# Loading x straight into the first transform's operand, at 128 elements a position instead of 130

## The chip, the cores and the metric

The kernel runs on one core of a Trainium2 chip. The metric is the device time of one execution in microseconds (us). The core has a matrix engine (TensorE, PE in the profile; its weight loads are PEld), VectorE (DVE), ScalarE (ACT), GpSimd (POOL) and SyncE (SP). In this kernel GpSimd and SyncE mostly issue DMA transfers.

## The reference

Two layers in a row, for x of 8 batches, 5696 positions and 128 channels. The first is a long convolution along the positions, the second a spectral mix of the first 64 modes, with a residual and a ReLU.

```python
L = 2 * S                                   # S = 5696
y = np.fft.irfft(np.fft.rfft(x, n=L, axis=1) * np.fft.rfft(h, n=L, axis=0)[None], n=L, axis=1)[:, :S]
X = np.fft.rfft(y, axis=1)                  # second layer, on y
Y[:, :64] = (Xr @ w_r - Xi @ w_i) + 1j * (Xr @ w_i + Xi @ w_r)    # for each mode
u = y + np.fft.irfft(Y, n=S, axis=1)
out = u + np.maximum(u @ w_ch, 0)
```

Inputs and output are float32; the kernel works in 16-bit floats (fp16) in its on-chip memory.

## The kernel before, in words

A sequence of 5696 positions is seen as 89 rows (`NQ`) of 64 positions (`J`). One row lies on one partition of the on-chip memory, so that partition q holds positions 64 q to 64 q + 63, with 128 channels each. The Fourier transform is split into a first transform over the 89 rows, done for each of the 64 places in a row, and a second one over the 64 places, done for each of 90 frequencies (`NK`). The batches are worked off in four pairs (`NP`).

The tile `Xin` (`x_sb`, L221) is the first transform's operand. It has 2 x 64 positions on each partition, and a position takes `XS = D + 2 = 130` elements: 128 channels and 2 unused ones.

The first transform of a pair is 32 calls of `a_tile` (L444). Each has four matmuls, and each matmul loads one channel of all 128 positions (two batches of 64) from Xin as its weights: 128 columns that lie `XS` elements apart. It then runs the 180 columns of the table `F1` through them. The results are evacuated into `As`, in turn by ScalarE and VectorE.

The second part of a pair is a loop of 26 ticks (`tick`, L619). Up to tick 22, each tick transforms four frequencies from As (`second`), multiplies them by the filter's spectrum on VectorE (`products`, tiles `U`), runs the inverse over the 64 places (weights `Wc`), evacuates to `Zs` or `Zt`, and stores to a scratch in device memory (`zscr`); the modes for the second layer are summed on the way (weights from Zs and Zt, table `G`). As becomes free from the front: after tick t, the part for that tick's frequencies is not read any more.

The next pair's x is loaded during the same loop. It comes in eight pieces (two batches, four pieces of 16 places, `XC = 4`), each as two DMA transfers from GpSimd's queue (9 rows and 80 rows; `x_load`, L353), which turn float32 into fp16. Piece i is issued in tick 2 (i + 1) (L638), after that tick's products and after the reads of As so far. It lands in a room `Xt` (`x_st`, L241), which lies over the part of As that has become free. Later, in the ticks that the table `XPLACE` gives (L611), VectorE copies each room into Xin (`x_place`, L360): 16 runs of 128 elements on 89 partitions, each run at a step of 130. The next pair's first transform begins in ticks 22 to 25 (six calls of `a_tile`, the table `border`, L528) and is finished after the loop (26 calls, L699).

The first pair's x lands in other rooms (`Xr`, L240) and is copied to Xin by the same `x_place` (L438) while the filter h is transformed. Its first transform is interleaved with the first matmuls of the filter's second transform (L680). The rows of Xin from partition 64 on are set to zero once at the start (L344).

Nobody writes waits by hand: every operation names what it reads and writes, and a recorder (L21) works out which operations on other queues it must wait for. A token such as `("xin", i)` stands for piece i of Xin. An engine works its own instructions off in the order in which they are recorded.

Of the kernel before, what the change touches and what calls it, by code (L numbers as in the profile page):

```python
# [4 lines left out]
P = 128  # L5
F16 = mybir.dt.float16
# [117 lines left out]
def bass_long_conv_fft__then__afno_spectral_mix_kernel(nc, x, h, moe_w_r, moe_w_i, moe_w_ch, out):  # L124
    B, S, D = x.shape
    M = moe_w_r.shape[0]
    assert D == P and M == 64 and B == 8
    J = 64
    NQ = S // J
# [3 lines left out]
    NP = B // 2  # L133
# [72 lines left out]
    def at(name, cols, dt, off):  # L206
        return nc.alloc_sbuf_tensor_at(name, [P, cols], dt, offset=off)

    def take(nbytes):
        off = (cur[0] + 31) // 32 * 32  # L210
        cur[0] = off + nbytes
        assert cur[0] <= end, (cur[0], end)
        return off

    AW, HW, GW = NK * 2 * D, NK * D, (NK // 2 + 1) * P
    a_as = take(AW * 2)
    a_sb = at("As", AW, F16, a_as)
    XS = D + 2
    XW = 2 * J * XS
    a_x = take(XW * 2)  # L220
    x_sb = at("Xin", XW, F16, a_x)  # L221
    a_m = take(MW * 2)
    m_sb = at("M", MW, F16, a_m)
# [5 lines left out]
    NU, NXS, NZ, NZX = 3, 2, 6, 10  # L229
# [7 lines left out]
    XC = 4  # L237
    XN = J // XC
    XB = XN * D
    x_all = at("Xr", 2 * XC * XB, F16, a_h)  # L240
    x_st = [at(f"Xt{i}", XB, F16, a_as + i * XB * 2) for i in range(2 * XC)]  # L241
    u_s = [at(f"U{i}", 2048, F16, a_st + i * 4096) for i in range(NU)]
    x_s = [at(f"Xs{i}", 1024, F16, a_st + NU * 4096 + i * 2048) for i in range(NXS)]
    z_s = [at(f"Zs{i}", 1024, F16, a_st + NU * 4096 + (NXS + i) * 2048) for i in range(NZ)] + \
# [1 line left out]
    f1_sb = at("F1", 2 * NK, F16, take(2 * NK * 2))  # L246
# [3 lines left out]
    xt = at("XT", B * XTW, F16, a_g + GW * 2 + 2048 * (NZX - NZ))  # L250
# [31 lines left out]
    def ap(t, row, p0, n, off, dims):  # L282
        return bass.AP(t, p0 * row + off, [[row, n]] + [list(d) for d in dims])
# [8 lines left out]
    R = Recorder(nc)  # L292
# [23 lines left out]
    def dma(eng, dst, src, ring, reads=(), writes=(), after=()):  # L316
        R.add(eng, lambda h_: h_.dma_start(dst, src), reads, writes, ring=ring, after=after)  # L317
# [32 lines left out]
        dma("gpsimd", bass.AP(h_in, o_, dims), bass.AP(h.tensor, h.offset + o_, dims), "x", (), [("hin", i)])  # L350
    HT = [("hin", i) for i in range(len(h_parts))] + [("hz",)]

    def x_load(g_, i, dst, toks, after=()):  # L353
        b, c_ = divmod(i, XC)
        for p_, (q0, n) in enumerate(((QA, NQ - QA), (0, QA))):
            dma("gpsimd", bass.AP(dst, q0 * XB, [[XB, n], [1, XB]]),
                bass.AP(x.tensor, x.offset + (2 * g_ + b) * S * D + q0 * J * D + c_ * XB, [[J * D, n], [1, XB]]),
                "x", (), [toks[p_]], after=after)

    def x_place(i, src, toks):  # L360
        R.add("vector", lambda e: e.tensor_copy(bass.AP(x_sb, i * XN * XS, [[XW, NQ], [XS, XN], [1, D]]),  # L361
                                                src),
              list(toks) + XZ, [("xin", i)])

    def w_pieces():
        out_ = []
# [10 lines left out]
    RA = 2 * XC * XB  # L377
# [8 lines left out]
            dma("gpsimd", bass.AP(x_all, (b_ * XC + c_) * XB, [[RA, QA], [1, XB]]),  # L386
                bass.AP(x.tensor, x.offset + b_ * S * D + c_ * XB, [[ROW, QA], [1, XB]]), "x", (), [("xr", b_ * XC + c_, 1)])
    XZ = [("xz",)]
    XIN = [("xin", i) for i in range(2 * XC)]
    XR = [[("xr", i, p_) for p_ in range(2)] + [("xl", 0), ("xl", 1)] for i in range(2 * XC)]  # L390
    MP = 6
    GP = 2 * KT
# [30 lines left out]
    for j in range(16):  # L423
        t = turns("h", [0, 2, 4])
        for i in range(4):
            d = 4 * j + i
            mm(pv(t + i // 2, (i % 2) * 2 * NK, [[1, 2 * NK]]),
               ap(hp_sb, 2 * J * HS, 0, P, d, [[HS, 2 * J]]), f1_sb[:, :], True, True,
               [("hz",), ("hp", d // DC), ("f1",)], [bank(t + i // 2)])
        for i in range(4 if j < 15 else 26):  # L430
            mm(pv(6 + i % 2, 0, [[1, 2 * NK]]), f1_sb[:, 0:P], f1_sb[:, :], True, True, [("f1",)], [bank(6 + i % 2)])
        evac(bass.AP(ah_sb, 4 * j, [[HW, P], [DH, 2 * NK], [2, 2], [1, 2]]),
             pv(t, 0, [[1, 2 * NK], [512, 2], [2 * NK, 2]]),
             [bank(t), bank(t + 1)], [("ah", j)], 1.0 / 64,
             eng="vector" if j in (3, 7) else "scalar")
        if j % 2:
            i = j // 2 % 2 * XC + j // 4
            x_place(i, bass.AP(x_all, i * XB, [[RA, NQ], [D, XN], [1, D]]), XR[i])  # L438

    HP = [("hz",), ("hp", 0), ("hp", 1)]  # L440
    AHT = [("ah", j) for j in range(16)]
    AST = [("as", j) for j in range(33)]

    def a_tile(j, slots, eng=None):  # L444
        t = turns("s", slots) if len(slots) > 1 else slots[0]
        for i in range(4):
            d = 4 * j + i
            mm(pv(t + i // 2, (i % 2) * 2 * NK, [[1, 2 * NK]]),
               ap(x_sb, XW, 0, P, d, [[XS, 2 * J]]), f1_sb[:, :], True, True,
               XIN + XZ + [("f1",)], [bank(t + i // 2)])  # L450
        if eng == "both":
            for i, e in enumerate(("vector", "scalar")):
                evac(bass.AP(a_sb, 4 * j + 2 * i, [[AW, P], [D, 2 * NK], [1, 2]]), pv(t + i, 0, [[1, 2 * NK], [2 * NK, 2]]),
                     [bank(t + i)], [("as", j + i)], 1.0 / 64, eng=e, after=once(("hp", j), HP))
            return
        evac(bass.AP(a_sb, 4 * j, [[AW, P], [D, 2 * NK], [2, 2], [1, 2]]),
             pv(t, 0, [[1, 2 * NK], [512, 2], [2 * NK, 2]]),
             [bank(t), bank(t + 1)], [("as", j)], 1.0 / 64, eng=eng, after=once(("hp", j), HP))
# [149 lines left out]
              bk + [("h", t, 0), ("h", t, 1, 0), ("h", t, 1, J)], [("u", i)])  # L608

    Z_OLD = [("ag", k) for k in range(NS, NS + 8 * (NZX - NZ))]  # L610
    XPLACE = [9, 10, 12, 15, 16, 18, 20, 22], [9, 10, 13, 14, 17, 18, 20, 22]  # L611

    def zroom(g_, s_):
        return (s_ - 2 * NZ) % NZX if g_ == 0 and s_ >= 2 * NZ else s_ % NZS[g_]

    def xtok(n):
        return [("xt", n, p_) for p_ in range(2)]

    def tick(g_, t):  # L619
        if g_ + 1 < NP:  # L620
            for i in range(2 * XC):
                if t == XPLACE[g_ > 0][i]:
                    x_place(i, bass.AP(x_st[i], 0, [[XB, NQ], [D, XN], [1, D]]), xtok(i))
        with_h = with_h_at(g_, t)
        if t < NT:
            of_two = t > 0 and twin(g_, t - 1)
            if not of_two:
                second(g_, t)
            products(g_, t, slot_of(g_, t))
            if twin(g_, t):  # L630
                second(g_, t + 1)
                if straight(g_, t):
                    copied(g_, t + 1, slot_of(g_, t + 1))
        drain = list(border[t]) if t in border and g_ + 1 < NP else []
        if drain and t >= NT:
            j, sl, e = drain.pop(0)
            a_tile(j, [sl], e)
        if g_ + 1 < NP and t % 2 == 0 and 0 < t <= 4 * XC:  # L638
            i = t // 2 - 1
            x_load(g_ + 1, i, x_st[i], xtok(i), [("u", t % NU)] + AST)  # L640
        if LC <= t < NT + LC:
            s_ = t - LC
            n = len(ticks[s_])
            i, zi = s_ % NU, zroom(g_, s_)
            zb = [turns("z", ZBANK) for b in range(2)]
            for b in range(2):
                for r in range(2):
                    mm(pv(zb[b], 0, [[1, n * D]]), (W1, W2)[r], u_s[i][:, r * 1024 + b * 512:r * 1024 + b * 512 + n * D],
                       r == 0, r == 1, [("u", i), ("wc",)], [bank(zb[b])])
                evac(bass.AP(z_s[zi], b * D, [[1024, P], [2 * D, n], [1, D]]),  # L650
                     pv(zb[b], 0, [[D, n], [1, D]]), [bank(zb[b])], [("zs", zi, b)], eng="scalar",
                     after=once(("zx", zi, b), Z_OLD) if zi >= NZ else ())
            zo = (g_ * NK + KT * s_) * P * 256
            dma("sync", bass.AP(zs, zo, [[256, P], [P * 256, n], [1, 256]]),
                bass.AP(z_s[zi], 0, [[1024, P], [256, n], [1, 256]]), "z",
                [("zs", zi, 0), ("zs", zi, 1)], [("zd", g_, s_)])
            if drain and t >= NT:
                j, sl, e = drain.pop(0)
                a_tile(j, [sl], e)
        if LM <= t < NT + LM:  # L660
            s_ = t - LM
            zi = zroom(g_, s_)
            for i, k in sorted(enumerate(ticks[s_]), key=lambda q: (s_ > 0 or q[1] != 1, q)):
                for b in range(2):
                    if k % 2:
                        o, off, n, sl = pv(MB, b * P, [[1, P]]), (k + 1) // 2 * P, P, (k + 1) // 2
                    else:
                        ms, off = even[k]
                        n, sl = 2 * len(ms), 0
                        dims = [[M, 2]] if len(ms) == 1 else [[ms[1] - ms[0], 2], [M, 2]]  # L670
                        o = pv(MB, b * P + ms[0], dims)
                    mm(o, z_s[zi][:, i * 256 + b * P:i * 256 + b * P + P], g_sb[:, off:off + n],
                       k == 1 and b == 0, k == NK - 1 and b == 1, [("g", sl // GP), ("zs", zi, b)], [bank(MB)])
        if drain and t < NT + LM - 1:
            j, sl, e = drain.pop(0)
            a_tile(j, [sl], e)
        if with_h:
            filter_tick(t + LH, [2, 3])
# [216 lines left out]
```

## Time and profile before

| what | value |
|---|---|
| three timed runs | 391.25, 392.1 and 393.78 us; median 392.1 us |
| span of the profiled execution, first to last instruction | 390.0 us |
| its own time beyond the span | not listed; the runs' median is 2.1 us above the span |
| mean granted TensorE clock | 0.981 of full speed |
| HBM read, written | 70.61 MB, 51.12 MB |

The span has these stages: loading and transforming h, and the first pair's first transform (to about 46 us); the first pair's ticks (to about 100 us); the second and the third pair (to about 156 and 212 us); the last pair's ticks (to about 263 us); and then the inverse transform with the second layer and the output.

In the views, a group of instructions is given as line, engine, operation, `out<-in` by the program's tile names, and the shape. The number after x counts them. In a timeline, the first number is the start in us and the second the duration in us of the instructions merged into the line; brackets give how long the engine was idle before, and what ended that.

### The profile page before, as it was taken

To read this page: it belongs to the slowest core of one execution; us is meant where nothing else is said; L and a number is where in the kernel's file an instruction comes from. 1 tells how busy PE (TensorE), PEld (TensorE's weight loads), DVE (VectorE), ACT (ScalarE), POOL (GpSimd) and SP (SyncE) were. 2 spreads that over 40 slices of the span, in tenths; PEclk is the share of its full clock that TensorE was granted. 3 is DMA by queue.
4 is the path that set the end of the run, shared out by engine and by line. 5 is a ranking of instruction groups with operands and counts; after the bars stand their busy time and mean duration, and the time that the engine had idled before them with its cause. 6 is when DMAs were issued, how large, how long until landed. Compare 5 with 4: busy or idle time off the path is not lost.

```text
span 390.0 us, 12484 instructions
## 1 busy us (share of the span) xinstructions
PE 363.7 (93%) x5346; PEld 280.4 (72%) x5346; DVE 304.9 (78%) x346; ACT 311.0 (80%) x489; POOL 84.3 (22%) x134
## 2 busy tenths in 40 slices
PE   7699999998989999989998989999999999999992
PEld 7597766654866666866666856668898988988871
DVE  3358789988998999998998997875437767777784
ACT  8278689888889998989996999995457676777783
POOL 8500013220453320643210411319300000000000
PEclk9899999999999999999999999998899999999997
DMA  7998559999598998999996849999999999999967
GB/s 146 184 284 327 143 98 257 272 253 281 93 138 188 225 254 235 98 129 198 226 260 193 86 134 383 301 337 394 405 400 394 418 405 409 405 406 379 360 276 287
DMA packets 87089, 103.94 MB, mean 267 GB/s; under 512 B 22823, under 2 KB 72615, under 8 KB 83563
## 3 DMA queue, kind: packets, MB, share of 16 engines
q1 hardware_dynamic: 62523, 67.73, 49.7%
q0 software_dynamic: 24512, 35.43, 43.5%
q8 instruction: 42, 0.69, 0.7%
q14 instruction: 12, 0.10, 0.1%
HBM read 70.61 MB, written 51.12 MB: 312 GB/s over the span
## 4 chain that ended last, share of the span: by engine, by line
PE 68%; DMA 9%; DVE 8%; ACT 8%; issue 3%; POOL 1%; SPq 0%; DVEq 0%; ACTq 0%; POOLq 0%
PE ps L320 68%; DMA Hin<-in_h_dram 3%; DVE As L314 2%; DMA Hs<-Hs 2%; DMA zscr<-Zs 2%; DMA Xt<-in_x_dram 2%; ACT As L310 2%; DVE U L599 2%; ACT Zs L308 1%; DVE U L607 1%; ACT Xs L308 1%; ACT R L829 1%; ACT Zt L308 1%; ACT UT L308 1%; DVE Hs L312 1%
## 5 line engine op out<-in xcount | busy, mean ns | idle before, releaser
L607 DVE TENSOR_TENSOR U<-Xs,Hs 128x2048 f16<-128x2048 f16 (+1 forms) x73 | 86.9, 1193 | 16.0 <-ACT Xs L308 11.3
L320 PE MATMUL ps<-U,Wc 128*128 128x512 f16 (+1 forms) x368 | 94.3, 376 | 1.2 <-DVE U L607 0.6
L308 ACT CAST Xs<-ps 128x1024 f16<-128x1024 f32 (+1 forms) x77 | 74.9, 977 | 12.3 <-PE ps L320 7.4
L308 ACT CAST Zs<-ps 128x512 f16<-128x512 f32 (+1 forms) x134 | 70.7, 597 | 4.1 <-PE ps L320 2.5
L830 DVE TENSOR_TENSOR O<-ps,R 128x512 f32<-128x512 f32 x81 | 52.5, 684 | 19.9 <-ACT R L829 12.5
L314 DVE TENSOR_SCALAR As<-ps 128x720 f16<-128x720 f32 x70 | 58.1, 884 | 6.7 <-PE ps L320 5.9
L829 ACT ACTIVATE R<-ps 128x512 f32<-128x512 f32 x96 | 50.9, 573 | 14.1 <-PE ps L320 13.7
L320 PE MATMUL ps<-F,Xin 128*128 128x180 f16 x512 | 53.8, 249 | 4.1 <-DVE Xin L361 1.9
L320 PE MATMUL ps<-As,M 64*128 64x128 f16 x1440 | 50.3, 217 | 4.5 <-DVE U L599 2.9
L320 PEld LDWEIGHTS ps<-F,Xin 128*128 128x128 f16 x512 | 44.5, 155 | 12.8 <-DVE As L314 3.6
L320 PE MATMUL ps<-WI,UT 128*128 128x256 f16 x360 | 51.8, 279 | 0.5 <-DVE O L830 0.4
L310 ACT ACTIVATE As<-ps 128x720 f16<-128x720 f32 (+1 forms) x61 | 45.8, 770 | 7.0 <-PE ps L320 5.7
L320 PEld LDWEIGHTS ps<-U,Wc 128*128 128x128 f16 x368 | 28.4, 97 | 30.7 <-ACT Zs L308 5.3
L317 POOL DMA_DIRECT2D Xt<-in_x_dram x48 | 25.9, 544 | 105.2 <-PE ps L320 100.3
L320 PEld LDWEIGHTS ps<-As,M 64*128 64x128 f16 x1440 | 40.6, 94 | 10.7 <-DVE U L599 3.6
L308 ACT CAST UT<-ps 128x712 f16<-128x712 f32 x40 | 30.0, 752 | 19.0 <-PE ps L320 18.1
L320 PEld LDWEIGHTS ps<-WI,UT 128*128 128x128 f16 x360 | 39.3, 152 | 4.2 <-issue 1.7
L320 PE MATMUL ps<-IBs,C 128*128 128x356 f16 x128 | 40.5, 326 | 0.6
L320 PEld LDWEIGHTS ps<-G,Zs 128*128 128x128 f16 x524 | 26.6, 96 | 15.0 <-ACT Zs L308 2.5
L607 DVE TENSOR_TENSOR U<-ps,Hs 128x2048 f16<-128x2048 f32 x15 | 34.2, 2283 | 0.0
L320 PE MATMUL ps<-G,Zs 128*128 128x128 f16 (+2 forms) x524 | 33.0, 192 | 0.1
L312 DVE CAST UT<-ps 128x712 f16<-128x712 f32 x24 | 21.4, 890 | 9.8 <-PE ps L320 9.8
(87 smaller groups left out, 510.4 us busy)
## 6 DMA issues: line engine op xcount, KB each, us to landing
out_dram<-O SPq DMA_DIRECT2D x39, 512.0 KB, 10.2
zscr<-Zs SPq DMA_DIRECT2D x64, 256.0 KB, 7.4
Xt<-in_x_dram POOLq DMA_DIRECT2D x24, 320.0 KB, 7.0
zscr<-Zt SPq DMA_DIRECT2D x24, 256.0 KB, 6.9
W<-wscr POOLq DMA_DIRECT2D x4, 1024.0 KB, 8.0
M<-cM POOLq DMA_DIRECT2D x5, 720.0 KB, 20.5
ZT0a<-zscr SPq DMA_DIRECT2D x3, 1024.0 KB, 13.1
Hs<-Hs SPq DMA_DIRECT2D x44, 64.0 KB, 5.9
```

The lines of the kernel that those rows point to most:

```text
L308: R.add(e, lambda h_: h_.copy(dst, src), reads, writes, after=after)
L310: R.add(e, lambda h_: h_.activation(dst, src, COPY, scale=scale), reads, writes, after=after)
L312: R.add(e, lambda h_: h_.tensor_copy(dst, src), reads, writes, after=after)
L314: R.add(e, lambda h_: h_.tensor_scalar_mul(dst, src, scale), reads, writes, after=after)
L317: R.add(eng, lambda h_: h_.dma_start(dst, src), reads, writes, ring=ring, after=after)
L320: R.add("tensor", lambda h_: h_.matmul(o, l, r, start=st, stop=sp), reads, writes)
L599: R.add("vector", lambda e, b=b, s_=s_: e.tensor_tensor(bass.AP(u_s[i], b * 512, [[2048, P], [1024, 2], [1, n * D]]), s_, hv, MULT), [tok, ...
L607: R.add("vector", lambda e: e.tensor_tensor(uv, src, hv, MULT), bk + [("h", t, 0), ("h", t, 1, 0), ("h", t, 1, J)], [("u", i)])
L829: R.add("scalar", lambda e: e.activation(rv, src_r, RELU), bk, [("r", i % NR)], after=once(("r", i % NR), G_ALL + XTT + [("y", 0), ("y", 1 ...
L830: R.add("vector", lambda e: e.tensor_tensor(ov, src_u, rv, ADD), bk + [("r", i % NR)], [key + (h_,)], after=once(key, old))
```

## The change

The rooms Xt, their tokens and the table XPLACE go. `x_load` writes the two transfers of a piece directly into Xin, whose positions are now 128 elements apart, so that the 16 positions of a piece are one run of 2048 elements on each partition. A load is issued in the same tick as before, after that tick's products; it no longer waits for the reads of As. It has to wait for the matmuls that read the old x, as the recorder finds. Each piece has two tokens in place of one, for its two transfers, so the first transform of the second to fourth pair waits for 16 transfers where it waited for VectorE's copies. The first pair's copies stay, with contiguous destinations. The memory that Xin takes, and the place of everything behind it, stays the same (512 bytes are left free).

```diff
-    XS = D + 2
-    XW = 2 * J * XS
-    a_x = take(XW * 2)
+    XW = 2 * J * D
+    a_x = take(XW * 2 + 512)
...
-    x_st = [at(f"Xt{i}", XB, F16, a_as + i * XB * 2) for i in range(2 * XC)]
...
-    def x_load(g_, i, dst, toks, after=()):
+    def x_load(g_, i, after=()):
         b, c_ = divmod(i, XC)
         for p_, (q0, n) in enumerate(((QA, NQ - QA), (0, QA))):
-            dma("gpsimd", bass.AP(dst, q0 * XB, [[XB, n], [1, XB]]),
+            dma("gpsimd", bass.AP(x_sb, q0 * XW + i * XB, [[XW, n], [1, XB]]),
                 bass.AP(x.tensor, x.offset + (2 * g_ + b) * S * D + q0 * J * D + c_ * XB, [[J * D, n], [1, XB]]),
-                "x", (), [toks[p_]], after=after)
+                "x", (), [("xin", i, p_)], after=after)
 
     def x_place(i, src, toks):
-        R.add("vector", lambda e: e.tensor_copy(bass.AP(x_sb, i * XN * XS, [[XW, NQ], [XS, XN], [1, D]]),
-                                                src),
-              list(toks) + XZ, [("xin", i)])
+        R.add("vector", lambda e: e.tensor_copy(bass.AP(x_sb, i * XB, [[XW, NQ], [1, XB]]), src),
+              list(toks) + XZ, [("xin", i, 0), ("xin", i, 1)])
...
-    XIN = [("xin", i) for i in range(2 * XC)]
+    XIN = [("xin", i, p_) for i in range(2 * XC) for p_ in range(2)]
...
-               ap(x_sb, XW, 0, P, d, [[XS, 2 * J]]), f1_sb[:, :], True, True,
+               ap(x_sb, XW, 0, P, d, [[D, 2 * J]]), f1_sb[:, :], True, True,
...
-    XPLACE = [9, 10, 12, 15, 16, 18, 20, 22], [9, 10, 13, 14, 17, 18, 20, 22]
...
-        if g_ + 1 < NP:
-            for i in range(2 * XC):
-                if t == XPLACE[g_ > 0][i]:
-                    x_place(i, bass.AP(x_st[i], 0, [[XB, NQ], [D, XN], [1, D]]), xtok(i))
...
-            x_load(g_ + 1, i, x_st[i], xtok(i), [("u", t % NU)] + AST)
+            x_load(g_ + 1, i, [("u", t % NU)])
```

## The prediction

> **What bounds the kernel now.** I read the profile in this order: the busy shares of the page, the groups of instructions kept apart by shape, the view of tile Xin, narrow stretches of the timeline, and a table by stage.
>
> ```profile
> PE 363.7 (93%) x5346; PEld 280.4 (72%) x5346; DVE 304.9 (78%) x346; ACT 311.0 (80%) x489; POOL 84.3 (22%) x134
> ```
> TensorE is busy for 93% of the span and VectorE for 78%. TensorE is the bound on average; VectorE matters only where TensorE waits for it.
>
> ```profile
> L320 PEld LDWEIGHTS ps<-F,Xin x512: 145/152/188, 28.7 to 222.6; 128*128 128x128 f16 x171
> L361 DVE COPY Xin<-Xt x24: 677/682/690, 66.5 to 206.6; 89x2048 f16<-89x2048 f16 x24
>   PE ps L320: 1.9, 3
> ```
> From the view of tile Xin (ns min/median/max; the last line, under "who waited for it", is us, times): the 24 copies that go are 24 x 0.682 = 16.4 us of VectorE, but TensorE waited for one only 3 times, 1.9 us in all. The change also touches 512 weight loads that read Xin.
>
> ```profile
> 126.41 1.21 DVE L607 TENSOR_TENSOR U<-Xs,Hs 128x2048 f16<-128x2048 f16 x1
> 127.54 0.68 DVE L361 COPY Xin<-Xt 89x2048 f16<-89x2048 f16 x1
> 128.15 1.22 DVE L607 TENSOR_TENSOR U<-Xs,Hs 128x2048 f16<-128x2048 f16 x1
> ...
> 131.25 2.28 DVE L607 TENSOR_TENSOR U<-ps,Hs 128x2048 f16<-128x2048 f32 x1
> ...
> 138.29 2.28 DVE L607 TENSOR_TENSOR U<-ps,Hs 128x2048 f16<-128x2048 f32 x1
> ```
> ```profile
> 228.64 2.28 DVE L607 TENSOR_TENSOR U<-ps,Hs 128x2048 f16<-128x2048 f32 x1
> ...
> 232.72 1.22 DVE L607 TENSOR_TENSOR U<-Xs,Hs 128x2048 f16<-128x2048 f16 x1 [0.67 <-ACT Xs L308]
> ...
> 235.83 2.28 DVE L607 TENSOR_TENSOR U<-ps,Hs 128x2048 f16<-128x2048 f32 x1
> ```
> Two stretches of VectorE's timeline (start us, us). The first is the second pair, with copies: four ticks take 138.29 - 131.25 = 7.04 us. The second is the last pair, which has no copies: 235.83 - 228.64 = 7.19, and its later rounds (235.83, 242.87, 249.91) 7.04. So in the middle of a pair the copies fill time in which VectorE would idle, and are worth nothing.
>
> ```profile
> 198.65 7.93 DMA Xt<-in_x_dram
> 206.58 0.02 issue
> 206.60 0.70 DVE Xin L361
> 207.30 0.05 issue
> 207.35 3.72 PE ps L320 x36
> ```
> The chain at the end of the third pair: the last piece of x lands, is copied, and only then does the first transform start. This is where a copy is on the path.
>
> ```profile
> 28.82 1.09 PE L320 MATMUL ps<-F,Xin 128*128 128x180 f16 x12
> ...
> 44.29 0.85 PE L320 MATMUL ps<-F,Xin 128*128 128x180 f16 x8 [0.38 <-DVE As L314]
> ```
> ```profile
> 103.39 0.15 PEld L320 LDWEIGHTS ps<-F,Xin 128*128 128x128 f16 x1 [0.23 <-DVE As L314]
> ```
> ```profile
> 103.43 0.26 PEld L320 LDWEIGHTS ps<-F,Xin 128*128 128x128 f16 x2
> ```
> The first transform. Twelve matmuls in 1.09 us, the last of them 0.241: one every (1.09 - 0.24) / 11 = 77 ns. After an idle moment the second load starts about 43 ns after the first (103.39, 103.43; rounded, from the trace's own times): one load of 128 columns takes up some 43 ns and hides under the 77 ns of the matmul before it.
>
> **The gain.** In three places TensorE stops waiting for a copy.
> - First pair: its work is done at 95.1 and it starts at 95.74 (0.43 us idle, and 0.60 before the load). The last x landed at 92.7, so I count 0.55. Inside this pair VectorE has the filter's evacuations too: its tick is 2.08 us without a copy (62.64 to 64.72) and 2.34 with one (64.72 to 67.06), five times in the crowded part, so 1.3 us at most; the ticks there also wait for ScalarE and for DMAs (0.89 and 1.03 us before U at 83.53 and 88.20), so I take 0.5 of it.
> - Second pair: idle 0.33 to 0.50 before 151.15; x landed at 149.6. I take 0.4.
> - Third pair: idle 1.12 before 207.35, x landed at 206.58. The copy's 0.70 goes. The two loads that a copy started beside took 1.28 and 1.29 us to issue against 1.04 to 1.06 for the others, so the last landing may come 0.25 earlier. I take 0.85.
>
> Sum 2.3 us; bounds 0.5 (the borders alone, if what follows is paced by ScalarE) and 4 (all idle time and all 1.3 us).
>
> **What costs nothing.** The loads stay on GpSimd's queue at the same ticks; GpSimd is released by U (ends 117.10, issue 117.66), not by the reads of As that fall away, so none starts earlier. The new wait for the last transform's matmuls (done at 111.1) was met 6 us before. Bytes and run lengths of the 48 transfers are the same, and nothing is moved past SP's queue. The first pair's eight copies lose their gaps: 0.68 us each either way, bounded by the h copy's rate (4096 elements in 1.226) at 0.61 and twice at 1.36; the last ends at 27.8, and the transform starts at 28.74, so its cover is 0.9 us. ScalarE's zeroing of Xin (7.12 us from 2.6) gets 1/65 shorter, hidden by the landing of h at 14.2.
>
> **A new wait.** The first transform of a pair must now know of 16 transfers instead of one copy. Waits that no instruction carries are separate ones of 51 ns on TensorE's queue, two semaphores in each: 8 x 0.051 = 0.41 us a pair. In the first two pairs all have landed 1.5 us before and TensorE's queue reads them ahead; in the third pair they stand behind the landing, in front of the 36 matmuls, and take back up to 0.4 of the 0.85. Ends: 0 and 1.2 us; I take 0.2, inside the rounding of the gain.
>
> **The step that decides: the pitch of the weight load.** Each of the 512 loads reads 128 positions that were 130 elements apart (260 bytes) and will be 128 (256 bytes).
>
> ```profile
> L320 PEld LDWEIGHTS ps<-WI,UT 128*128 128x128 f16 x352 | 38.4, 153 | 3.0 <-ACT R L829 1.1 <-issue 0.8 <-ACT UT L308 0.2
> L320 PEld LDWEIGHTS ps<-U,Wc 128*128 128x128 f16 x368 | 28.4, 97 | 30.7 <-ACT Zs L308 5.3 <-ACT Zt L308 1.8 <-DVE U L599 1.0
> L310 ACT ACTIVATE As<-ps 128x720 f16<-128x720 f32 x58 | 44.4, 781 | 7.0 <-PE ps L320 5.7
> ```
> (Busy us, mean ns.) Neighbouring columns (Wc) load in 97 ns; columns 88 bytes apart (UT) in 153, 132 bytes (Hp) in 156, 260 bytes (Xin) in 152 to 155. So the time of a load depends on where its columns lie. The strides that the trace shows fall on 32, 64 and 64 different places within 256 bytes; the new one puts all 128 columns on a single place. No load in the trace does that. [...]
>
> Bounds from rows. Low end: 43 ns, as 260 bytes. High end: the one walk in 256-byte steps that the trace has is the write of As, 180 groups in 781 ns, 4.3 ns a step; it is paced by ScalarE, so a store part is free again after 4.3 ns at most, and 128 columns one by one would take at most 128 x 4.3 = 552 ns. The nearest row by distance is the low one (260 bytes), the nearest by pattern the high one. Between ends 13 times apart I take the middle by ratio: sqrt(43 x 552) = 154 ns.
>
> With L the spacing of loads in us, if L is over about 0.105:
> - First stage: 30 tiles of four matmuls took 44.29 - 28.82 = 15.47 us; they would take 120 L + 6 x 0.34 for the filter's matmuls between them, and two more tiles 8 (L - 0.077): 128 L - 14.05 more.
> - Three times, 26 tiles after the tick loop: 10.64 us now (100.45 to 111.09), paced by evacuations of 0.90 and 0.78 us; then 104 L each: 312 L - 31.9 more.
> - Three times, 24 matmuls among the last ticks: 24 (L - 0.077), less 0.3 us of idle time there: 72 L - 6.5 more.
>
> Together 512 L - 52.4. At 0.154 that is 26.4 us (5.7, 16.1, 4.6). Below 0.105 the matmuls and evacuations cover the loads and the cost is under 1.5 us.
>
> Sum against the profiled execution: 390.0 + 26.4 - 2.3 = 414.1 us of span. The runs' median is 392.1, 2.1 above that span; with it, **416.2 us**.
>
> [...]
>
> **Rivals.**
> 1. *The pitch makes no difference (not slower).* Strides of 88, 132 and 260 bytes all load in 152 to 156 ns: once columns lie apart, how far apart has not mattered. In steps of 260 bytes, neighbours already sit almost 256 apart. Against it: none of these rows has all columns on one place. It decides below L = 0.105, where 128 columns take no more than 105 ns. Then 392.1 - 2.3 = 389.8 us. [...]
> 2. *Faster by over 1%.* The first pair would have to give over 2 us: its ticks wait for DMA landings of 8.2 and 8.7 us, which could shorten when GpSimd issues undisturbed. But GpSimd's own queue takes 43.5% of the DMA engines' time over the span, and its bytes stay. 387 us.
> 3. *The columns are read wholly one by one,* L towards 0.552: 512 x 0.552 - 52.4 = 230 us more, about 620 us. Nothing but the upper bound speaks for it.
>
> **How the numbers follow.** A measurement of this kernel can tell about 1% (3.9 us) from no change. Pitch matters, L from 0.12 to 0.22: 0.50 (396 to 450 us, the likeliest one's own range). No difference, or one that stays hidden: 0.34, of which 0.30 within 1%. Rival 2: 0.04 (part of those 0.34). L over 0.22: 0.12. Something else that makes it slower by more than 1%, such as later landings: 0.04. The range reaches from 389 to 450 (L = 0.22: 512 x 0.22 - 52.4 - 2.3 = 57.9), and leaves 0.12 + 0.04 out. Faster 0.04, same 0.30, slower 0.66.
>
> **What would show it.** In the profile after, the Xin loads' mean ns above 155 and the 12 matmuls at 28.8 in about 12 x 0.154 = 1.85 us instead of 1.09; 26 tiles in 16 us instead of 10.6; ticks of the second and third pair still 7.04 us per four; TensorE's idle time before 95.7, 151.1 and 207.3 gone or behind waits on DMAs. If the matmuls still come every 77 ns, the deciding step is wrong and rival 1 stands.

## The result and the profile after

| | runs | median, us | lowest to highest, us | span of the profiled execution, us |
|---|---|---|---|---|
| before | 4 | 392.94 | 391.25 to 395.89 | 390.0 |
| after | 4 | 408.21 | 407.47 to 411.42 | 405.7 |

The changed kernel takes 1.0385 times as long (95% interval 1.0322 to 1.0448): it is slower by 15.3 us. The forecast was 416.2 us, with a range from 389 to 450.

The first part of the page after (busy us, share of the span, instructions):

```profile
PE 379.5 (94%) x5346; PEld 300.3 (74%) x5346; DVE 299.6 (74%) x322; ACT 325.2 (80%) x489; POOL 88.0 (22%) x134
```

VectorE has lost its 24 copies but only 5.3 us of work, though the copies were 16.4 us. ScalarE, whose instructions are the same 489, is busy 14.2 us longer, TensorE 15.8. So something else became longer, and the view of tile Xin after says what (ns min/median/max; at the end us, times):

```profile
L318 PEld LDWEIGHTS ps<-F,Xin x512: 208/245/325, 28.2 to 238.8; 128*128 128x128 f16 x171
L318 PE MATMUL ps<-F,Xin x512: 240/288/405, 28.2 to 238.9; 128*128 128x180 f16 x171
...
  DVE As L312: 12.0, 23
  ACT As L308: 7.0, 12
```

Before, the loads took 145/152/188 ns. TensorE waits for a copy only once, 0.7 us for the last one of the first pair, but the evacuations to As now wait 19.0 us for these matmuls, against 11.6.

The duration of one load (245 ns in the median) isn't the pitch of the loads, because they overlap. The pitch comes from the timeline of the weight loads, here the first twelve after:

```profile
28.16 1.54 PEld L318 LDWEIGHTS ps<-F,Xin 128*128 128x128 f16 x12 [0.93 <-issue]
```

and before:

```profile
28.74 1.01 PEld L320 LDWEIGHTS ps<-F,Xin 128*128 128x128 f16 x12
```

One load every (1.54 - 0.21) / 11 = 121 ns, where it was (1.01 - 0.15) / 11 = 78. The matmuls no longer hide the loads. In the stretch of 26 tiles that follows the first pair's ticks, the table by stage says the same (window; length; then busy us and count of PE, PEld, DVE, ACT, POOL; granted clock; DMA share; GB/s). After, then before:

```profile
106.60:119.94 13.34, 13.33 (x107) 13.18 (x108) 11.68 (x14) 11.58 (x15) 9.17 (x11) 1.00 0.87 87
```
```profile
100.45:111.26 10.81, 10.49 (x107) 9.03 (x108) 10.50 (x13) 10.13 (x15) 7.71 (x11) 1.00 0.96 102
```

PEld goes from 9.03 of 10.81 us to 13.18 of 13.34: the loads fill the stage. 104 loads in 13.34 us are one in 128 ns. The granted clock is full in both.

The groups by shape after show two things that the prediction doesn't have (busy us, mean ns of one | idle before, and what ended it):

```profile
L604 DVE TENSOR_TENSOR U<-Xs,Hs 128x2048 f16<-128x2048 f16 x69 | 84.2, 1223 | 28.0 <-ACT Xs L306 19.6 <-DMA Hs<-Hs 6.2 <-PE ps L318 1.8
...
L312 DVE TENSOR_SCALAR As<-ps 128x720 f16<-128x720 f32 x67 | 62.8, 945 | 14.6 <-PE ps L318 12.0
L308 ACT ACTIVATE As<-ps 128x720 f16<-128x720 f32 x58 | 53.3, 923 | 11.3 <-PE ps L318 7.0
```

The same evacuations took 781 ns on ScalarE before and take 923. On VectorE they took 900, as the line of before shows, and take 945, mostly because six among the last ticks take 1333 to 1362.

```profile
L314 DVE TENSOR_SCALAR As<-ps 128x720 f16<-128x720 f32 x67 | 56.7, 900 | 6.7 <-PE ps L320 5.9
```

And VectorE waits 6.2 us for `Hs<-Hs`, the DMAs that copy the filter's spectrum from one half of the partitions to the other. Before, it waited for them once, 0.26 us.

The stages, in us, as the matmuls on Xin and the first U of each pair mark them: a stage of the transform ends with the end of its last matmul on Xin, the 24 matmuls with the start of the 25th (three numbers: after the first, second and third pair's ticks):

| stage | before | after |
|---|---|---|
| first pair's first transform | 16.32 | 21.65 |
| ticks, U of tick 0 to the next transform's first matmul | 48.64, 38.42, 39.21 | 48.41, 38.34, 38.34 |
| 24 matmuls among the last ticks | 4.70, 4.71, 4.71 | 6.53, 6.46, 6.47 |
| 26 tiles after the ticks | 10.81, 10.81, 10.81 | 13.34, 13.31, 13.35 |
| last pair's ticks | 38.01 | 38.01 |

The stages of the first transform have grown by 5.3 + 5.3 + 7.6 = 18.2 us; the ticks have given 0.2 + 0.1 + 0.9 = 1.2. What lies outside the table (the start and the inverse transform) differs by another 1.3 us.

### The profile page after: what moved, and what is told of

It reads as the page before. It is cut to its first block, busy times and chain, and to the rows that moved or that the text cites. A ratio compares the mean times of both kernels' runs of the same rounds, so it can differ in the third digit from the quotient of the medians.

```text
span 405.7 us, 12439 instructions
## 1 busy us (share of the span) xinstructions
PE 379.5 (94%) x5346; PEld 300.3 (74%) x5346; DVE 299.6 (74%) x322; ACT 325.2 (80%) x489; POOL 88.0 (22%) x134
## 2 busy tenths in 40 slices
DMA packets 87089, 103.94 MB, mean 256 GB/s; under 512 B 22823, under 2 KB 72615, under 8 KB 83563
## 4 chain that ended last, share of the span: by engine, by line
PE 67%; DMA 10%; ACT 9%; DVE 8%; POOL 2%; issue 2%; SPq 0%; DVEq 0%; ACTq 0%; POOLq 0%
PE ps L318 67%; DMA zscr<-Zs 4%; DMA Xr<-in_x_dram 4%; DVE As L312 3%; ACT As L308 3%; DVE U L596 2%; POOL Xr L315 2%; DMA Hs<-Hs 2%; DVE U L604 1%; ACT Hs L306 1%; ACT Zs L306 1%; ACT R L818 1%; ACT Xs L306 1%; ACT UT L306 1%; POOL Hin L315 1%
## 5 line engine op out<-in xcount | busy, mean ns | idle before, releaser
L604 DVE TENSOR_TENSOR U<-Xs,Hs 128x2048 f16<-128x2048 f16 (+1 forms) x73 | 89.5, 1229 | 28.7 <-ACT Xs L306 20.3
L306 ACT CAST Zs<-ps 128x512 f16<-128x512 f32 (+1 forms) x134 | 73.2, 620 | 2.9 <-DMA zscr<-Zs 2.1
L312 DVE TENSOR_SCALAR As<-ps 128x720 f16<-128x720 f32 x70 | 64.2, 928 | 14.6 <-PE ps L318 12.0
L318 PE MATMUL ps<-F,Xin 128*128 128x180 f16 x512 | 71.4, 292 | 3.4 <-DVE As L312 1.6
L318 PEld LDWEIGHTS ps<-F,Xin 128*128 128x128 f16 x512 | 66.6, 248 | 8.4 <-DVE As L312 4.7
L308 ACT ACTIVATE As<-ps 128x720 f16<-128x720 f32 (+1 forms) x61 | 54.3, 901 | 11.3 <-PE ps L318 7.0
L315 POOL DMA_DIRECT2D Xin<-in_x_dram x48 | 25.0, 526 | 110.5 <-DVE U L604 57.7
L306 ACT CAST Zt<-ps 128x512 f16<-128x512 f32 (+1 forms) x50 | 27.8, 627 | 0.5 <-PE ps L318 0.5
```

What stands on the lines that cost most here:

```text
L306: R.add(e, lambda h_: h_.copy(dst, src), reads, writes, after=after)
L308: R.add(e, lambda h_: h_.activation(dst, src, COPY, scale=scale), reads, writes, after=after)
L312: R.add(e, lambda h_: h_.tensor_scalar_mul(dst, src, scale), reads, writes, after=after)
L318: R.add("tensor", lambda h_: h_.matmul(o, l, r, start=st, stop=sp), reads, writes)
L604: R.add("vector", lambda e: e.tensor_tensor(uv, src, hv, MULT), bk + [("h", t, 0), ("h", t, 1, 0), ("h", t, 1, J)], [("u", i)])
```

## The experiments

The leading theory, P, is that the pitch of 128 elements makes the weight loads slower and the rest hardly counts. Against it stood W, that the landing, with its new waits and other transfers, is what costs. The probes then ask whether the pitch is slow by itself (A) or only beside other work, and which pitches are.

**The pitch alone.** The kernel before, with its rooms and copies, but 128 elements a position.

```diff
-    XS = D + 2
+    XS = D
     XW = 2 * J * XS
-    a_x = take(XW * 2)
+    a_x = take(XW * 2 + 512)
```

> The kernel before with one edit: Xin's positions are 128 elements apart instead of 130; rooms and copies stay. Theory P (the pitch of the weight loads costs all of it): 392.9 + 15.3 + the gain of the landing that is missing here (2.3) = 409 to 412 us, matmuls of the first transform about 130 ns apart, as in the changed kernel. Rival W (landing straight in Xin costs it, by later transfers or by the 16 waits): 392 to 394 us, matmuls 77 ns apart.

Measured: 411.68 us against 393.45, a ratio of 1.0432 (1.0368 to 1.0496). Its view of tile Xin:

```profile
L320 PEld LDWEIGHTS ps<-F,Xin x512: 208/246/324, 29.9 to 243.3; 128*128 128x128 f16 x171
...
L361 DVE COPY Xin<-Xt x24: 679/683/696, 73.4 to 223.1; 89x2048 f16<-89x2048 f16 x24
```

The copies are all there, and the loads are as long as in the changed kernel. The pitch by itself costs 18.2 us, more than the whole change, and the time is the one that P expected. W falls.

**The landing alone.** The changed kernel, whose transform reads its columns at a step of 130 elements all the same. The data lie at 128, so it transforms other columns than it should; the work is the same. The spare end of Xin's rows, which is read now, is cleared at the start (not shown here).

```diff
-    XW = 2 * J * D
-    a_x = take(XW * 2 + 512)
+    XW = 2 * J * (D + 2)
+    a_x = take(XW * 2)
...
-               ap(x_sb, XW, 0, P, d, [[D, 2 * J]]), f1_sb[:, :], True, True,
+               ap(x_sb, XW, 0, P, d, [[D + 2, 2 * J]]), f1_sb[:, :], True, True,
```

> The changed kernel, but the weight loads step 130 elements through data that lies at 128, so they read wrong columns and the output is not the reference's; only the time counts. All of the landing is in, the pitch is not. Theory P: 389.5 to 392 us (the predicted gain of 2.3 against before), matmuls 77 ns apart. Rival W: about 408 us.

Measured: 389.13 us against 393.45, a ratio of 0.9865 (0.9811 to 0.9919), slightly below the range that P expected. The view of tile Xin has the old loads again:

```profile
L318 PEld LDWEIGHTS ps<-F,Xin x512: 145/152/185, 28.6 to 219.1; 128*128 128x128 f16 x171
```

The stages of the first transform are those of before within 0.1 us each, and the ticks take 46.22, 38.37 and 38.50 us, so they give 2.4, 0.05 and 0.7. In the first pair VectorE's timeline shows how (start us, us):

```profile
66.61 1.23 DVE L605 TENSOR_TENSOR U<-Xs,Hs 128x2048 f16<-128x2048 f16 x1 [0.25 <-ACT Xs L306]
67.75 0.68 DVE L310 CAST Hs<-ps 128x512 f16<-128x512 f32 x1
68.69 1.22 DVE L605 TENSOR_TENSOR U<-Xs,Hs 128x2048 f16<-128x2048 f16 x1 [0.25 <-ACT Xs L306]
...
79.09 1.22 DVE L605 TENSOR_TENSOR U<-Xs,Hs 128x2048 f16<-128x2048 f16 x1 [0.25 <-ACT Xs L306]
```

A tick every 2.08 us from 56.21 to 79.09, without exception: 22.88 us for eleven, where before they took 23.82 (56.40 to 80.22). The other 1.5 us come between 79 and the transform's start, where before VectorE was still copying. The third pair's start, where the copy was on the path:

```profile
203.46 0.69 DVE L605 TENSOR_TENSOR U<-Xs,Hs 128x1024 f16<-128x1024 f16 x1 [0.24 <-ACT Xs L306]
203.91 0.69 PEld L318 LDWEIGHTS ps<-F,Xin 128*128 128x128 f16 x8 [0.55 <-issue]
203.94 0.82 PE L318 MATMUL ps<-F,Xin 128*128 128x180 f16 x8 [0.40 <-issue]
```

TensorE is idle for 0.40 us before it, ended by nothing but its own queue ("issue"): there its separate wait instructions stand. The trace of the changed kernel, which has the same landing, shows eight of them in each of the first three pairs, 51 ns long and most of them 0.106 us apart; in its third pair the last four start from 218.95 to 219.26, while the weight loads stand still (0.39 us). The last x transfer of this pair was issued at 195.7 here, and none takes over 7.4 us to land, so x is there by 203.1 and it isn't the landing that TensorE waits for. The second pair has 0.28 us of the same idle time, where it had 0.33 with the copy, and so gains next to nothing. The first pair has none.

**Which pitches are slow.** Bursts of 24 loads of 128 columns from Xin, put ahead of the first transform of the changed kernel, with matmuls of only 16 columns behind each load and the other engines idle. Every burst has another step. (Xin's rows are a little longer here than in the changed kernel, and cleared to their end.) This kernel and the next ran once each; only the bursts in their traces are read, not their times.

```diff
...
+    for pitch in (1, 8, 44, 66, 130, 128, 129, 127, 126, 124, 120, 112, 96, 64, 32, 16, 128, 130):
...
+        for i in range(24):
+            mm(pv(6 + i % 2, 0, [[1, 16]]), ap(x_sb, XW, 0, P, i, [[pitch, 2 * J]]), f1_sb[:, 0:16], True, True,
...
```

> The changed kernel with bursts of 24 weight loads from Xin put ahead of the first transform, each with a matmul of only 16 columns, at steps of 1 to 130 elements, while ScalarE and VectorE stand still. The spacing in a burst is the time that a load takes up by itself. Theory A (columns on one place within 256 bytes are slow by themselves): about 128 ns at a step of 128, 43 at 130. Theory B (loads and the evacuations' writes to As, which walk in 256-byte steps at the same low address, hinder each other): at 128 the same 43 ns as at 130, the slowness appears only beside evacuations. The other steps show the law: if the number of different places within 256 bytes decides, 64 (2 places), 96 and 32 (4) and 112 (8) lie between.

From the timeline of the weight loads; the steps of these seven lines are 1, 8, 130, 128, 129, 96 and 64 elements:

```profile
28.18 0.67 PEld L318 LDWEIGHTS ps<-F,Xin 128*128 128x128 f16 x24 [0.71 <-DVE Xin L359]
...
29.03 1.55 PEld L318 LDWEIGHTS ps<-F,Xin 128*128 128x128 f16 x24
...
34.79 1.69 PEld L318 LDWEIGHTS ps<-F,Xin 128*128 128x128 f16 x24
36.84 3.01 PEld L318 LDWEIGHTS ps<-F,Xin 128*128 128x128 f16 x24
40.20 1.60 PEld L318 LDWEIGHTS ps<-F,Xin 128*128 128x128 f16 x24
...
52.20 1.67 PEld L318 LDWEIGHTS ps<-F,Xin 128*128 128x128 f16 x24
54.23 2.28 PEld L318 LDWEIGHTS ps<-F,Xin 128*128 128x128 f16 x24
```

| step, elements | mean time from load to load, ns |
|---|---|
| 1 | 25 |
| 8, 16, 32, 44, 66, 96, 112, 120, 124, 126, 127, 129, 130 | 61 to 67 |
| 64 | 90 |
| 128 (first and second burst) | 120, 121 |

The table by stage (columns as above) has the two bursts that decide, at 130 and at 128 elements:

```profile
34.70:36.50 1.80, 1.80 (x28) 1.80 (x27) 0.00 (x0) 0.00 (x0) 0.00 (x0) 0.50 0.92 378
36.80:39.90 3.10, 3.10 (x28) 3.10 (x27) 0.00 (x0) 0.00 (x0) 0.00 (x0) 0.50 0.05 15
```

No other engine works beside them, so A holds: a load at 128 is slow by itself, 120 ns against 67 at 130. DMAs were still moving data during the first five bursts (share 0.92 and more), but hardly beside the first one at 128 (0.05), and not at all from 40.2 to 42.0 and from 54.2 to 56.5 us (0.00). The second bursts at 128 and 130, later still, took 121 and 66 ns. So DMAs aren't the cause. The grading that the theory expected for 96, 112 and 32 elements isn't there. Steps of 32 and 96 elements (64 and 192 bytes) put the 128 columns on four places within 256 bytes and cost nothing (61 to 67 ns); 64 elements leave two places (90 ns), 128 one (120). After the first two bursts the granted clock fell to 0.50. The bursts at 130 and 128 both ran at 0.50, so they compare; and the one at 8 elements, at full clock, took 61 ns against 67 at 130 with a clock of 0.50, so the clock seems to matter little to a load.

**Wider pitches.** The same bursts, with steps up to 180 elements, reading from the memory of As (cleared ahead), which is large enough for them.

```diff
...
+    for pitch in (128, 130, 132, 136, 144, 160, 176, 180, 64, 128):
...
```

> The changed kernel with bursts of 24 weight loads at steps of 128, 130, 132, 136, 144, 160, 176, 180 and 64 elements from a cleared part of the memory of As, ahead of the first transform, with other engines still. If only steps that are whole multiples of 128 bytes collide: 120 ns at 128, 88 at 64, and about 60 at all others. If any multiple of 32 or 64 bytes collides: 144 (288 bytes), 160 (320) and 176 (352) are above 60 too.

Steps of 128, 130, 144 and 160 elements:

```profile
40.80 2.96 PEld L318 LDWEIGHTS ps<-F,Xbig 128*128 128x128 f16 x24 [12.09 <-DVE Xbig L671]
44.12 1.73 PEld L318 LDWEIGHTS ps<-F,Xbig 128*128 128x128 f16 x24
...
50.31 1.68 PEld L318 LDWEIGHTS ps<-F,Xbig 128*128 128x128 f16 x24
52.34 1.68 PEld L318 LDWEIGHTS ps<-F,Xbig 128*128 128x128 f16 x24
```

130, 132, 136, 144, 160, 176 and 180 take 64 to 69 ns, 64 takes 90, and 128 takes 119 twice. Of all steps tried, from 2 to 360 bytes, only the two that are multiples of 128 bytes are slow.

**Xin moved by 128 bytes, then by 32.** The changed kernel, Xin a little further on. The pitch stays; what changes is which addresses of Xin and As agree in their low bits. As has been written, all along, in steps of 256 bytes too, and it lies right ahead of Xin with a length of 180 x 256 bytes, so that without the move both begin at the same low address.

```diff
-    x_sb = at("Xin", XW, F16, a_x)
+    x_sb = at("Xin", XW, F16, a_x + 128)
```

In the second kernel it is `a_x + 32`.

> The changed kernel with Xin moved by 128 bytes, so that its columns no longer share the low address bits with the place in As that is being written. Theory A: no change, 407 to 409 us, and evacuations still stretched. Theory B: back towards 391 to 394 us, evacuations again 0.78 and 0.90 us.

> The changed kernel with Xin moved by 32 bytes instead of 128. If the evacuations were hindered because loads and writes of As met in the same 16 or 32 bytes of every 256, this distance is enough: ScalarE's evacuations back at 0.78 us and 404 us in all, as with 128 bytes. If the places that hinder each other are wider than 32 bytes, the evacuations stay at 0.87 and the time at 408 us. Spacing of the matmuls about 130 ns in either case.

Moved by 128 bytes: 403.85 us, ratio to before 1.0253 (1.0175 to 1.0331). By 32: 406.74 us, 1.0374 (1.0316 to 1.0433). Groups by shape, by 128 bytes:

```profile
L318 PEld LDWEIGHTS ps<-F,Xin 128*128 128x128 f16 x512 | 66.5, 248 | 4.3 <-DVE As L312 1.7 <-ACT As L308 1.1 <-issue 0.9
L312 DVE TENSOR_SCALAR As<-ps 128x720 f16<-128x720 f32 x67 | 60.4, 908 | 14.8 <-PE ps L318 11.9
L308 ACT ACTIVATE As<-ps 128x720 f16<-128x720 f32 x58 | 45.4, 787 | 13.9 <-PE ps L318 13.8
```

and by 32:

```profile
L312 DVE TENSOR_SCALAR As<-ps 128x720 f16<-128x720 f32 x67 | 60.6, 913 | 14.4 <-PE ps L318 11.6
L308 ACT ACTIVATE As<-ps 128x720 f16<-128x720 f32 x58 | 45.1, 782 | 14.5 <-PE ps L318 14.3
```

The loads are as slow as before the move (248 ns), but the evacuations are back to 782 to 787 and 908 to 913 ns. So the stretch of the evacuations depends on the addresses of Xin and As: 923 ns where the low bits agree, 787 and 782 once Xin is moved, 781 at the old step. The loads' own time doesn't, 248 ns on average in all three kernels with the pitch of 128. Neither of the two outcomes expected for the move by 128 bytes came: the evacuations are free, as theory B has it, but the loads and most of the time stay. For 32 bytes the evacuations came out as expected for narrow places; the time by the runs did not. In the profiled executions the 24 matmuls among the last ticks take 5.72, 5.67 and 5.36 us instead of 6.5, the first stage 20.65 instead of 21.65, the 26 tiles the same. By the spans, the moves gain 3.3 and 2.7 us. By the runs, the first gains 4.4 and the second 1.5, but the intervals of both overlap the changed kernel's (1.0322 to 1.0448), the first one's barely. So the gain in time is not certain; the stages and the evacuations show it.

**The landing at a step of 130.** Rival S keeps the landing and the spare elements: the DMA itself writes runs of 256 bytes at a step of 260.

```diff
...
-            dma("gpsimd", bass.AP(x_sb, q0 * XW + i * XB, [[XW, n], [1, XB]]),
-                bass.AP(x.tensor, x.offset + (2 * g_ + b) * S * D + q0 * J * D + c_ * XB, [[J * D, n], [1, XB]]),
+            dma("gpsimd", bass.AP(x_sb, q0 * XW + i * XN * XS, [[XW, n], [XS, XN], [1, D]]),
+                bass.AP(x.tensor, x.offset + (2 * g_ + b) * S * D + q0 * J * D + c_ * XB, [[J * D, n], [D, XN], [1, D]]),
...
```

> The changed kernel with the pitch of 130 kept: the transfers land straight in Xin, but in runs of 128 elements at a step of 130, so every run of 4096 bytes becomes sixteen of 256. It computes the reference's output. Theory P with cheap small runs: 388 to 391 us, as where only the landing was changed, and better than both kernels. Rival S (small runs cost more than the copies did): the x transfers take clearly longer than 7 us to land or to issue, the ticks of the first pairs wait for them and for the others on the same engines, and the time is 395 us or more.

Measured: 423.03 us against 392.97, a ratio of 1.0785 (1.0731 to 1.084), worse than the change. The DMA packets of the page after and of its own page, and its view of tile Xin:

```profile
DMA packets 87089, 103.94 MB, mean 256 GB/s; under 512 B 22823, under 2 KB 72615, under 8 KB 83563
DMA packets 121649, 103.95 MB, mean 247 GB/s; under 512 B 59519, under 2 KB 109311, under 8 KB 118123
```
```profile
L319 PEld LDWEIGHTS ps<-F,Xin x512: 145/152/187, 28.7 to 253.4; 128*128 128x128 f16 x171
...
L316 POOL DMA_DIRECT2D Xin<-in_x_dram x48: 610/770/945, 54.4 to 220.6; - x48
...
  DMA Xin<-in_x_dram: 51.0, 6
...
DMA to landing us min/median/max: 2.7/9.9/19.0
```

The loads are fast. But the packets went from 87089 to 121649, all of the growth under 512 bytes; an issue takes 770 ns on GpSimd in place of 529 after the change, a transfer lands after 9.9 us in place of 6.0, and engines wait for x (51.0 us in the sum over them). The ticks take 56.2, 49.1 and 45.0 us. Rival S holds: the copies that the change took out are the cheaper way to spread the positions.

**The copies on GpSimd.** Rival G: the kernel before, with the 24 copies moved from VectorE to GpSimd.

```diff
...
-                    x_place(i, bass.AP(x_st[i], 0, [[XB, NQ], [D, XN], [1, D]]), xtok(i))
+                    x_place(i, bass.AP(x_st[i], 0, [[XB, NQ], [D, XN], [1, D]]), xtok(i), "gpsimd")
```

> The kernel before (rooms, copies, pitch of 130), with the 24 copies of later pairs on GpSimd's queue instead of VectorE's. It computes the reference's output. If the copies' price was VectorE's time in the first pair and at the ends of the pairs, and GpSimd copies a piece in under about 2 us: 389 to 391 us, as with the landing alone. Rival G: a copy takes several us on GpSimd, holds up the loads behind it on that queue or the products that read on-chip memory beside it, and the time is 394 us or more.

Measured: 412.75 us against 391.89, a ratio of 1.0556 (1.0459 to 1.0654). From its view of tile Xin:

```profile
L361 POOL COPY Xin<-Xt x24: 1887/1934/2914, 67.6 to 222.7; 89x2048 f16<-89x2048 f16 x24
```

A copy takes 1.93 us there, 2.8 times VectorE's 0.68, and the next x loads are issued on the same queue behind it. The ticks take 49.7, 49.5 and 44.3 us. Rival G holds too.

None of the kernels that do the whole work beats the one before. The landing alone, 389.1 us, shows about what could be had if x could land without a copy and be read at a harmless step.

## Why the prediction was right, and where its sizes were off

**The mechanism.** The direction and the deciding step held. The prediction bet that columns which all agree in their low address bits load slower than any in the trace of before; alone, this costs 18.2 us, and the bursts show it with no other engine at work. Rival 1, no difference, falls, and with it the argument that 88, 132 and 260 bytes already load alike: those steps are all among the harmless ones (61 to 67 ns in the bursts). Rival 3 falls too: 120 ns are far from 552. Rival 2 does not come about, though the landing alone is faster by 1.35% (0.9865, interval 0.9811 to 0.9919): the landing can't be had without the pitch.

**"Pitch of the weight load", L.** This is the term that was mis-sized: 154 ns taken, 128 measured in the 26 tiles, 120 in the bursts. The bounds were poor at both ends. The 43 ns came from one pair of loads after an idle moment; 24 in a row at the old step come every 67 ns. The 552 ns, an estimate from the pace of ScalarE's writing, were four times too high. The middle by ratio landed near by luck: from 67 it would have been 192. (One figure of the prediction doesn't follow from its formula: its likeliest case, L from 0.12, begins at 399 us and not at 396.)

The prediction's reason, that few places within 256 bytes remain, is borne out only roughly. Four places (32 or 96 elements) cost nothing, two 1.35 times and one 1.8 times the 67 ns. What makes the steps of 64 and 128 elements slow, no run shows.

**The formula** keeps its form. At L = 0.128 its three lines give

- first stage 128 x 0.128 - 14.05 = 2.3 us; measured 5.3
- three times 26 tiles 312 x 0.128 - 31.9 = 8.0; measured 7.6
- three times 24 border matmuls 72 x 0.128 - 6.5 = 2.7; measured 5.3

so 13.1 us, and not 18.2. The 26 tiles, where the loads fill the stage, come out. The other two lack that evacuations stretch: the same evacuation by ScalarE takes 781 ns beside loads at 260 bytes, 923 beside loads at 256, and 787 once Xin is moved. With Xin moved by 128 bytes the border matmuls cost 5.72 + 5.67 + 5.36 - 14.12 = 2.6, the formula's figure. The first stage still costs 4.3 there: ScalarE's five evacuations to Hs in it take 1221 ns on average, against 579 before, and so don't follow this move. Whether they are what makes up the rest of the first stage was not tried. That the forecast's first stage (5.7) and border (4.6) look right is chance: a load 26 ns too slow stood in for the stretch that it did not have.

**The gain of the landing.** Taken as 2.3 us (1.05 in the first pair, 0.4, 0.85). At the old step the ticks give 2.4 + 0.05 + 0.7 = 3.2. The first pair was under-read: I counted 0.55 at its end and 0.5 of the crowded ticks' 1.3 us; with the whole of that it would have been 1.85, and 2.4 came. The second was over-read: the new wait instructions stand where the copy was waited for, with 0.28 us of idle time there and 0.40 in the third pair. The prediction had them read ahead in the first two pairs, which held in the first alone (in the changed kernel they start there from 98.93 to 99.67, and the matmuls ahead of the transform run to 100.24). It also priced them at 0.051 us each, their own duration; the pitch is mostly 0.106, and in the trace of before two of them already start 0.106 us apart (265.22 and 265.33). There are eight of them a pair, as it had them, but the 0.2 us for all pairs was too little.

In the changed kernel the gain is smaller: 0.2 + 0.1 + 0.9 = 1.2. Part of the difference is the pitch's, not the landing's: with the pitch alone the ticks take 48.96, 38.43 and 39.59 us, in the first and third pair longer than before, and against them the landing gains 0.5 + 0.1 + 1.3 = 1.9. The loss is in the first pair, and VectorE's timeline after shows where:

```profile
76.37 1.23 DVE L604 TENSOR_TENSOR U<-Xs,Hs 128x2048 f16<-128x2048 f16 x1 [1.10 <-DMA Hs<-Hs]
...
83.54 1.23 DVE L604 TENSOR_TENSOR U<-Xs,Hs 128x2048 f16<-128x2048 f16 x1 [1.04 <-DMA Hs<-Hs]
...
97.60 3.77 DVE L604 TENSOR_TENSOR U<-Xs,Hs 128x2048 f16<-128x2048 f16 x3 [2.05 <-DMA Hs<-Hs]
```

The tick waits for the copy of the filter's spectrum to the other half of the partitions, five times, 6.2 us (7.5 us with Xin moved by 128 bytes, 3.4 by 32, 2.0 in the kernel with the pitch alone, none in the one with the landing alone). At the first of these waits the transfer was not issued late: it starts 15.9 us after the pair's first U, with the landing alone 16.1. It takes 8.8 us in place of 6.9 (7.5 at most with the landing alone). What makes it slower is not settled.

**The sum.** 390.0 + 26.4 - 2.3 was 414.1 of span. L takes off 13.3, what the formula's terms lack puts on 5.1, the smaller gain 1.1, and the start and the end of the kernel differ by -1.3: 405.7, as profiled. The moves of Xin show that the stretched evacuations to As make up 2.7 us of the 5.1 among the last ticks and 1.0 us in the first stage. The rest is open.

**What costs nothing** did cost nothing as far as the stages show it: the last pair's ticks are 38.01 us in both, and the eight copies of the first pair, without their gaps, take 686 ns against 682.

## What to carry to other kernels

Before taking spare elements out of a layout, ask who reads it along the other axis. Two spare elements in 130 kept 128 columns off one low address and hid 512 loads under their matmuls; without them each load cost 120 ns instead of 67 in the bursts. Work taken off an engine is worth only the places where someone waits for it: 16.4 us of copies were worth 3.2 us alone by the stages (4.3 by the runs), and 1.2 in the changed kernel.

## What the runs showed of the hardware that was not expected

- Of the column steps tried from 2 to 360 bytes, only 128 and 256 bytes slow a load of 128 fp16 columns (90 and 120 ns, against 61 to 69 at steps from 16 bytes on and 25 for neighbouring columns); 64, 192, 288 and 320 bytes don't.
- Loads at a step of 256 bytes also go with longer writes elsewhere in the store: ScalarE's 128x720 evacuation went from 781 to 923 ns, six of VectorE's from about 900 to about 1350. Moving the tensor by 32 or 128 bytes frees nearly all of both (787 and 782 ns on ScalarE, 908 and 913 on average on VectorE, where 945 were), without making the loads faster (248 ns each). A U of 128x1024 that starts beside the first loads takes 1.57 us in place of 0.68; the move did not free it (up to 1.64).
- The load at 256 bytes took 120 ns alone and 128 in the kernel; where the other 8 come from was not tried.
- The bursts' spacing at 128 elements (120 ns, at a granted clock of 0.50) is the same as in the first twelve loads of the changed kernel (121 ns), though its clock was full: at this step the clock of TensorE hardly shows in it.
